# A new task list for the first thousand steps of an RWKV-7 + GELU kernel

## The chip, the cores and the metric

The kernel runs on one core of one Trainium2 chip, in one launch. The metric is the device time of that core in microseconds (us); lower is better.

## The reference

Two blocks follow each other. First an RWKV-7 recurrence over 768 time steps, for 4 batches x 8 heads of width 40, all in float32; then its output, as 3072 tokens of width 320, goes through a feed-forward block with a quick GELU between two matrix products (320 to 2048 and back).

```python
for t in range(S):                       # S = 768; B, H, D = 4, 8, 40
    y[:, :, t] = einsum('bhd,bhde->bhe', r_t, state)
    Sa = einsum('bhde,bhe->bhd', state, a_t)
    state = state * w_t - outer(Sa, b_t) + outer(v_t, k_t)
x = y.transpose(0, 2, 1, 3).reshape(B * S, H * D)
h = x @ w_in                             # 320 x 2048
out = (h / (1 + exp(-1.702 * h))) @ w_out  # 2048 x 320
```

## The kernel before

The time axis is cut into 12 chunks of 64 steps, and the four batches into two pairs. A chunk of one pair is a *unit*; there are 24, numbered 0 to 23, and units 2c and 2c+1 make up chunk c. Within a unit the recurrence becomes matrix products, and the work goes through these stages, all of them named by the tiles that they write:

- `decay(i)`: logarithms of the decays on ACT, sums over time as matmuls into `ps_cum` and `ps_cumc`, exponentials `FT`, `GT`, `wch`, `G` on ACT.
- `prep(i)`: the inputs `ak`, `b` and `time` are scaled by these (the results `ak`, `b`, `kh`, `bh`), on DVE or POOL; scores `A` and `RV` by matmul and a masked read out of PSUM on DVE.
- `inverse(i)`: a triangular inverse in five *levels*. For units 0 to 3 (`plain_level`), each level is a matmul into `ps_level`, a copy of the result `PT<-ps_level` (L792, ACT or DVE) and a transpose of the same PSUM tile `EX<-ps_level` (L729, DVE). Both must be done before the next level's matmul. Then come `ps_Q`, `QT`, `ps_T` and the inverse `T`.
- `solve(i)`: `ps_X`, the masked `M<-ps_X` (L915, DVE), `ps_y`; the new state `zraw` and the output `zr`; `x<-zr,FT` (L961, DVE or POOL). For units from 2 on, the state of unit i-2 enters through `zr<-zraw,wz`, `ps_zT` and `ps_rz`.
- `part_with` and `get_back` (L971, L975): `x` goes to DRAM and returns, turned, as `xT_all`.
- `mlp(c)`, once both units of chunk c are back: four groups q of ten steps `ps_up` (L300, 64x256 matmuls), a GELU `g<-ps_up` (L996, ACT) for each group, and for each of the two units eight steps `ps_down`.

The feed-forward weights come in eight blocks of 1.31 MB, each in four loads (L469), and each block is put through five steps before use: one on ACT (`rebased`, L447), three on DVE (`bounded` L451, `shifted` L455, `rounded` L459) and one on POOL (`joined`, L463). Blocks 0 to 3 are `w_in`: group q of chunk 0 waits for block q. Blocks 4 to 7 are `w_out`: steps 2n and 2n+1 of `ps_down` need block 4+n.

Nothing of the order is left to a scheduler. Every piece of work is a task with a number, the engines that may do it, a cost in ns on each of them (with the order written out these costs decide nothing, but they can be summed over a stretch of a list) and, where it uses PSUM, a pair of banks; `ORDER` is a text that lists all 2700 tasks, each with a letter for the engine (p TensorE, a ACT, d DVE, g POOL, s SyncE) and the number of its PSUM pair (0 to 3). `Plan.listed` reads it and the tasks are then issued one after the other, so each engine has its instructions in the order of the list:

```python
n, bank = one.split(ENGINES[e])
t = self.tasks[int(n)]
assert e in t.engines and t.after <= done and (e == "SP" or (t.pair is None) == (not bank))
t.engine, t.bank = e, int(bank or 0)
```

Every matmul of the kernel is recorded under one line (L300, a helper), so that TensorE's work is told apart by tile names. DMAs are all issued by SyncE, in the order of the list; a load of a unit's input waits there until the buffer of unit i-2 is free.

Of the kernel before, what the change touches and what calls it, by code (L numbers as in the profile page):

```python
# [119 lines left out]
214p1 389p2 66d 472a3 483g 204p0 390a2 560s 371p3 67d 306a 53s 215p1 71s 482s 216p1 372a3 217p1 476a 220p2 373d3 68g 218p1  # L120
221p2 477d 219a1 205p0 222p2 206p0 223p2 224p2 207p0 55a 311p3 225p2 79s 312d3 80s 226p2 208a0 58d 313p1 374p3 314d1 227p2 56d
379a3 228p2 229p2 57d 326p0 230a2 59g 393p1 327d0 378a3 391p2 394a1 375d3 231p0 558s 392d2 376a 232p0 233p0 395d1 559s 81s 73a
78s 234p0 480s 381p2 235p0 328p1 481s 382a2 74d 377a3 485d 380a3 236p0 75d 492a 242p2 486d 243p2 82a 76d 484d 77g 383p3 237p0
384d3 244p2 329d1 330d1 488p3 473d 238p0 531d 245p2 487g 246p2 489d3 85d 532p1 239p0 533a1 396p3 331d 332s 474s 475s 534a1
240p0 247p2 397d3 562s 241a0 535p1 83d 490p3 536a1 84d 398p0 572a 491d3 86g 550p1 555s 561s 253p3 399d0 551a 333s 400d0 254p3
401d 402s 554s 255p3 552a1 564d 493p0 705s 556a 567g 570p1 403s 494d0 248p2 563d 566g 249p2 495d0 498d 256p3 571d1 565g 250a2
496a0 251d2 252s 696p1 497g 557d 539p0 537p2 704s 257p3 538a2 540d0 258p3 553d 611d 697a 499d 573p2 784s 700s 259p3 576a2
574d2 710d 260p3 541d0 575d2 404p0 578d 261a3 577g 405p0 579d 698a1 568p2 711g 500p1 406p0 569d2 501a1 407p0 262d3 263s 708s
580p2 702a 502d1 408p0 582d2 409p0 503d 410p0 583d 504a 612p3 411p0 584g 613d3 412p0 614d3 413p0 505p1 709d 414a0 426p3 506d1
427p3 428p3 507d1 429p3 699d 581d2 430p3 615p1 785s 706s 701s 703d 431p3 616a1 585p0 432p3 508d 586a0 433p3 587d0 434p3 509a  # L130
588d 435p3 589d 448p2 436a3 510p1 590p0 511a1 449p2 592d0 591a0 512d1 415p3 513d 416p3 593d 514a 417p3 594g 418p3 515p0 419p3
516a0 517d0 595p1 518d 420p3 596a1 597d1 421p3 598d 422p3 519a 599d 423p3 424p3 520p0 425a3 437p1 521d0 438p1 523d0 522g 439p1
524d0 440p1 525d0 441p1 442p1 526d0 527p3 718p0 929s 528a3 443p1 719d0 787s 444p1 720d0 529p3 445p1 721d0 446p1 530d3 600p0
723d 447a1 542p3 722d 724g 603d0 605a0 619p1 604d0 543d3 450p2 620a1 606d0 544p3 621d1 601d0 602d 617p1 707s 546d3 451p2 618a1
783s 712d 547g 713d 607p0 725p1 608a0 452p2 609p0 453p2 548s 610d0 932s 454p2 727d1 726d1 622p0 728d 545d3 729a 775p1 455p2
623d0 780s 776a 549s 756d 730p3 624p0 456d2 457d2 731d3 458s 459p2 777a1 778g 732d3 786s 788g 781a 779s 626d0 460p2 625d0 627g
733d 795p1 835d 734a 461p2 735p3 791g 462p2 628s 736a3 796d1 737d3 716p0 792g 738d 463p2 782d 739g 1011s 920p1 757p3 925s
464p2 717d0 758a3 629s 759a3 790d 465p2 740p0 789d 466p2 741a0 742d0 921a 797p3 467d2 760p0 1008s 468d2 800a3 923d 652p2 469s
761d0 922a1 653p2 926a 930s 798d3 714p1 799d3 654p2 924s 802d 801g 655p2 934d 803a 656p2 836p0 657p2 715d1 658p2 659p2 837d0
762p3 838d0 927d 660p2 763a3 661p2 764p1 662a2 743d 630p0 744d 928s 631p0 632p0 765d1 804p3 766d1 633p0 805a3 806d3 634p0 807d  # L140
635p0 808a 745p2 636p0 748d2 637p0 749d2 839p1 933g 750d2 638p0 840a1 1009s 751d2 639p0 809p3 746d2 935g 640a0 641p1 810d3
642p1 793p2 747a 811d3 674p0 812d 794d2 813a 752p3 643p1 753a3 814p2 644p1 815a2 816d2 754p3 645p1 755d3 646p1 817d 647p1 818a
767p2 841p3 768d2 648p1 842a3 649p1 819p2 650p1 820a2 821d2 675p0 769p3 822d 651a1 823d 771d3 931s 770d3 772g 824p2 936d 676p0
827a2 828a2 942p1 829a2 677p0 1153s 830a2 937d 945a1 773s 663p3 825d2 664p3 943d1 1156s 826a 665p3 944d1 999p2 947d 946g 666p3
1000a 1004s 980d 940p1 948g 667p3 941d1 668p3 774s 669p3 670p3 831p1 671p3 1001a2 1002d 1003s 832d1 672p3 1005a 1013d 678p0
673a3 1006d 833p2 843p1 679p0 834d2 1007s 844d1 938p2 845d1 680p0 939d2 846p3 681p0 847d3 949p1 1012g 682d0 848p2 950a1 683d0
1014d 684s 685p3 849d2 1015g 1010s 850d2 1021p0 1016g 951d1 686p3 1024a0 1232s 851d 1235s 981p2 687p3 982a2 952d 852s 1022d0
983a2 953g 1144p1 1023d0 688p3 1026d 1145a 1149s 1025d 1027g 984p2 1059d 689p3 1154s 954p0 853s 985a2 1147g 690p3 1158d 1148s
955a0 956d0 986p2 1146a1 957d 1150a 691p3 958d 987a2 1151d 988p0 692p3 989a0 1152s 990d0 959p1 693a3 865p2 960a1 694d3 866p2
961d1 867p2 695s 962d 868p2 963d 1028p0 869p2 1029a0 1030d0 870p2 1031d 1157g 871p2 1159d 1032a 1060p3 872p2 873p2 1061a3  # L150
874p2 1062d3 1033p1 875a2 854p0 1035d1 855p0 1036d 856p0 1037d 1063p3 857p0 1064d3 1034a1 858p0 964p2 859p0 965a2 966d2 1038p1
967d 860p0 1039a1 1040d1 861p0 1041d 1017p3 968a 1042g 862p0 1018d3 863p0 969p2 864a0 876p1 970d2 877p1 972d2 971g 1043p3
973d2 878p1 1044a3 974d2 879p1 975d2 880p1 881p1 1045d3 1019p0 1046d 976p2 1047a 882p1 1020d0 1233s 883p1 977a2 1166p3 884p1
1169a3 1167d3 1377s 978p0 885p1 1168d3 898p2 1171d 1170g 886a1 979d0 887p3 1172a 1048p0 991p1 1051a0 888p3 1052a0 992d1 889p3
1053a0 890p3 1054a0 891p3 1049d0 993p1 1050a 1067p0 994d1 1160g 1155s 892p3 1161d 1068a0 893p3 894p3 1069d0 1380s 895p3 1204d
1065p0 995d1 896p3 996d 1066a0 1231s 1055p1 899p2 897a3 1056d1 997s 1173p0 1223p3 900p2 1174a0 1175d0 1228s 1176d 1224a 1177g
1057p1 901p2 1058d1 1070p0 998s 1164p1 1225a3 1226d 1236g 1227s 1071d0 902p2 1229a 1165d1 1162p3 903p2 1238d 1163d3 904p2
1237d 1178p0 1230d 905p2 1179a0 1180d0 1245p1 906a2 1181d 1072p3 1248a1 1456s 907d2 1182g 1246d1 908s 1247d1 909p0 1250d 1234s
1239g 1073d3 1251a 910p0 1240g 1074d3 1249d 1183p2 1459s 1283d 1368p1 911p0 1184a2 1075d 1373s 912p0 1185d2 1369a 1076s 1186d
# [978 lines left out]
```

## Time and profile before

| | |
|---|---|
| median of 3 runs | 678.03 us (677.79 to 678.33) |
| span of the profiled execution, first to last instruction | 676.5 us |
| PE (TensorE matmul) busy | 648.5 us, 96% of the span |
| DVE, ACT, POOL busy | 444.6, 331.6, 175.3 us |
| bytes moved by DMA | 69.74 MB, 103 GB/s over the span |

The page gives the span alone for the profiled execution; the runs' median is 1.5 us above it, and this much is taken to lie around the span. PE's matmuls overlap in the array and their ends are modelled, so that a busy share of 96% is no statement on the array's use; PE's idle time, on the other hand, is real. "issue" as the end of a wait means that the profile shows nothing that was waited for. All line numbers are those of the kernel before.

### The profile page before, as it was taken

The page shows a single profiled execution, that of the slowest core. Times are in us where ns is not written, and L with a number is a line of the kernel's source. Part 1 is how long each engine was busy: PE and PEld are TensorE (multiplying, and loading weights), DVE is VectorE, ACT ScalarE, POOL GpSimd, SP SyncE. Part 2 cuts the span into 40 slices and gives each one's busy share as a digit, 9 for nine tenths or more (in the row PEclk, how much of TensorE's full clock was granted, in tenths as well). Part 3 has the DMA queues.
Part 4 walks back from the last instruction along what each step waited for, and adds up shares of the span by engine and source line. Part 5 has one row for each costly group of instructions (what it writes and reads, how often), then busy time and mean ns, then how long its engine had stood idle before and what let it go on. Part 6 is the DMA issues. An engine that isn't in the chain of part 4 may idle for free.

```text
span 676.5 us, 42217 instructions
## 1 busy us (share of the span) xinstructions
PE 648.5 (96%) x19488; PEld 553.4 (82%) x19488; DVE 444.6 (66%) x908; ACT 331.6 (49%) x710; POOL 175.3 (26%) x204
## 2 busy tenths in 40 slices
PE   5768999999999999999999999999999999999997
PEld 5657887987998987788888888798888798798785
DVE  4786787777867667767776587768656766675001
ACT  4676755534564655664545445455454354252110
POOL 6344244224123123123123211322412421300000
PEclk9899999999999999999999999999999999999999
DMA  7983736315314314432404413513412411200200
GB/s 230 300 289 94 232 107 187 103 43 154 108 47 149 93 58 117 121 108 72 118 22 132 141 34 109 156 33 108 140 39 71 122 53 54 61 14 15 61 12 20
DMA packets 35313, 69.74 MB, mean 103 GB/s; under 512 B 5440, under 2 KB 14656, under 8 KB 35136
## 3 DMA queue, kind: packets, MB, share of 16 engines
q1 hardware_dynamic: 35136, 67.03, 32.6%
q8 instruction: 153, 2.51, 1.5%
q14 instruction: 24, 0.20, 0.1%
HBM read 59.15 MB, written 7.86 MB: 99 GB/s over the span
## 4 chain that ended last, share of the span: by engine, by line
PE 93%; DMA 2%; DVE 2%; issue 1%; ACT 1%; DVEq 0%; SPq 0%; ACTq 0%
PE ps_up L300 31%; PE ps_down L300 30%; PE ps_level L300 9%; PE ps_y L300 5%; PE ps_B L300 5%; PE ps_X L300 2%; PE ps_N L300 2%; PE ps_rz L300 2%; PE ps_RV L300 2%; PE ps_A L300 2%; PE ps_zT L300 1%; DMA ak<-in_ak 1%; PE ps_cum L300 1%; PE ps_T L300 1%; DMA b<-in_b 1%
## 5 line engine op out<-in xcount | busy, mean ns | idle before, releaser
L300 PE MATMUL ps_up<-xT_all,w_sb 64*64 64x256 f32 x3840 | 251.0, 377 | 0.8 <-issue 0.4
L300 PE MATMUL ps_down<-w_sb,g 64*64 64x320 f32 x3072 | 237.0, 430 | 0.2 <-ACT zr L877 0.2
L300 PEld LDWEIGHTS ps_up<-xT_all,w_sb 64*64 64x64 f32 x3840 | 170.1, 133 | 15.9 <-issue 1.5
L300 PEld LDWEIGHTS ps_down<-w_sb,g 64*64 64x64 f32 x3072 | 128.0, 133 | 42.8 <-ACT zr L877 0.4
L996 ACT ACTIVATE g<-ps_up 128x1024 f32<-128x1024 f32 x48 | 49.2, 1024 | 45.4 <-PE ps_up L300 45.0
L715 POOL TENSOR_TENSOR EX<-ES,quads 128x512 f32<-128x512 f32 x29 | 38.3, 1322 | 112.7 <-DVE ES L708 74.9
L300 PEld LDWEIGHTS ps_level<-W,EX 64*64 64x64 f32 x2560 | 57.8, 134 | 6.7 <-DVE T L838 0.5
L758 ACT COPY W<-ps_level 128x512 f32<-128x512 f32 (+1 forms) x56 | 29.5, 527 | 67.7 <-PE ps_level L300 65.7
L760 DVE TENSOR_TENSOR E<-two,ps_level 128x256 f32<-128x256 f32 x80 | 33.1, 415 | 34.2 <-ACT W L758 30.1
L300 PE MATMUL ps_level<-W,EX 64*64 64x64 f32 (+1 forms) x2560 | 55.4, 217 | 0.1
L713 ACT ACTIVATE EX<-ES,quads 128x256 f32<-128x256 f32 x80 | 36.3, 501 | 31.0 <-DVE ES L708 30.3
L619 POOL TENSOR_TENSOR ak<-ak,FT 128x512 f32<-128x512 f32 x16 | 20.9, 1305 | 76.6 <-DMA ak<-in_ak 53.4
L708 DVE STREAM_TRANSPOSE ES<-E 128x256 f32<-128x256 f32 x80 | 35.3, 443 | 4.4
L300 PE MATMUL ps_level<-PT,EX 64*64 64x64 f32 (+2 forms) x1280 | 32.8, 235 | 5.1 <-DVE EX L729 3.7
L300 PEld LDWEIGHTS ps_level<-PT,EX 64*64 64x64 f32 x1280 | 30.8, 139 | 8.3 <-DVE EX L729 4.2
L300 PE MATMUL ps_y<-M,bh 64*64 64x104 f32 (+1 forms) x768 | 35.6, 250 | 0.7 <-DVE M L915 0.4
L300 PE MATMUL ps_y<-RV,kh 64*64 64x104 f32 (+1 forms) x768 | 35.6, 251 | 0.0
L899 ACT COPY B<-ps_B 128x416 f32<-128x416 f32 (+1 forms) x34 | 16.6, 492 | 33.4 <-PE ps_B L300 33.2
L300 PEld LDWEIGHTS ps_y<-RV,kh 64*64 64x64 f32 x768 | 28.3, 137 | 2.6 <-DVE M L915 0.5
L689 DVE COPY_PREDICATED PT<-within,ps_N 128x256 f32<-128x256 uint32 x40 | 17.8, 444 | 18.5 <-ACT P L697 13.5
L915 DVE TENSOR_TENSOR M<-ps_X,later 128x832 f32<-128x832 f32 (+1 forms) x24 | 23.8, 993 | 8.3 <-PE ps_X L300 8.1
L300 PE MATMUL ps_B<-RV,A 64*64 64x104 f32 (+1 forms) x768 | 27.9, 252 | 1.1 <-issue 1.1
(131 smaller groups left out, 1088.2 us busy)
## 6 DMA issues: line engine op xcount, KB each, us to landing
ak<-in_ak SPq DMA_DIRECT2D x48, 160.0 KB
rv<-in_rv SPq DMA_DIRECT2D x48, 160.0 KB
time<-in_time SPq DMA_DIRECT2D x24, 320.0 KB
xT_all<-x_dram SPq DMA_DIRECT2D x48, 160.0 KB
wc<-in_wc SPq DMA_DIRECT2D x20, 264.0 KB
logw<-in_w SPq DMA_DIRECT2D x24, 160.0 KB
RV<-in_v SPq DMA_DIRECT2D x24, 160.0 KB
b<-in_b SPq DMA_DIRECT2D x48, 80.0 KB
```

The lines of the kernel that those rows point to most:

```text
L300: nc.tensor.matmul(o, lhsT, rhs, start=start, stop=True, skip_group_check=True)
L619: plan.add(R, {"DVE": 690.0, "POOL": 1270.0, "sbuf": True}, lambda t: of(t.engine).tensor_mul(ahT(), ahT(), FT_of(i)), reads=T("ak", "FT") ...
L689: plan.add(R, dve(256), lambda t, n=n: nc.vector.copy_predicated(tiles_of(at(E0_t, i)), every(within_of(n), [128, 2, 4, 32]), blocks(psum( ...
L708: plan.add(rank, dve(256), lambda t: nc.vector.transpose(ES(n), source(t)), writes=[key("ES", n, 6)], **reads)
L713: nc.scalar.activation(dst[:, :, h], ES(n), ACT.Copy, scale=quads[:, h, :1])
L715: of(t.engine).tensor_mul(dst, ES(n).unsqueeze(2).to_broadcast([128, 8, 2, 32]), quads.unsqueeze(1).to_broadcast([128, 8, 2, 32]))
L758: plan.add(rank, any2(512 - 8 * past), lambda t: copy(t.engine)(tiles_of(W(n + 1))[:, :, :, past:], blocks(psum(t, ""), 64)[:, :, :, past: ...
L760: plan.add(rank, dve(256), lambda t: nc.vector.tensor_sub(tiles_of(E(n + 1)), every(two32, [128, 2, 4, 32]), blocks(psum(t, ""), 64)[:, :, ...
L899: plan.add(R, any2(4 * wide), lambda t: copy(t.engine)(dst(), some(psum(t, "")[:, :, :208])), writes=[("Bv", i)] if x and c > 0 else T("B" ...
L915: plan.add(R + 1, dve(8 * wide), lambda t: nc.vector.tensor_tensor(M_of(i)[:, :, :wide].rearrange("p (j b) n -> p b j n", b=2), some(psum( ...
L996: plan.add(-45, {"ACT": 1030.0, "table": "gelu"}, lambda t: nc.scalar.activation(g_of(c * NQ + q).rearrange("p m r n -> p r m n"), psum(t, ...
```

## The change

Only the text `ORDER` differs; the tasks, their instructions and the code that issues them are the same. In the list:

- the first 999 of the 2700 entries are a new order of the same 999 tasks; the remaining 1701 are the same tasks on the same engines in the same order;
- 120 of the first 999 tasks are on another engine: 52 from ACT to DVE, 32 from DVE to ACT, 15 from DVE to POOL, 12 from POOL to DVE, 8 from ACT to POOL, 1 from POOL to ACT;
- the PSUM pairs of the first part are given out anew; in the rest, pairs 1, 2 and 3 are renamed to 2, 3 and 1 throughout;
- the SyncE entries move too, so the loads come in another order. Of the weights' 32 loads, 19 stood ahead of `ps_y` of unit 1 (entry 192p) and 9 do now; ahead of the first `ps_up` (entry 209p) 22 stood and 11 do.

The text has seven lines more, so a line below it is found seven lines further down (the matmul helper L300 is L307 there). The beginning of both lists, up to unit 0's first levels (matmuls 107p, 110p; copies `PT` 108, 111; transposes `EX` 109d, 112d):

```diff
-0s 5s 7s 8s 9s 3a 6s 87p0 88p1 24s 89a1 1s 2s 12s 102a 95d 100p2 90a0 93d 158a 101d2 98p3 96g 10s 94d 17s 97g 16s 99d3 103p1
-4a 11s 132p0 104a1 105d1 142p2 26s 143p3 133a0 106d 130p1 14s 144a3 13s 107p0 15s 18s 151g 108a0 109d0 51s 131a1 110p3 27s
-149g 150d 111a3 112d3 159p0 156p1 145a2 161d0 160a0 152g 113p3 345s 92a 162d 25s 153d 114a3 163p2 42s 115d3 34s 19a 274s 264p0
...
+0s 3a 87p2 88p3 89a3 90a2 158a 102a 9s 96g 5s 97g 93d 95d 7s 6s 100p0 8s 94d 101d0 1s 98p3 11s 18s 99d3 103p2 105d2 4a
+143p0 106d 142p1 10s 14s 144a0 149g 107p3 151g 104a2 108d3 109d3 145a1 2s 153g 110p3 150d 152g 111d3 112d3 159p2 161d2
```

In the old list `ps_y` of unit 1 is 192p, and 194a (`zr`), 195g (`x`), 196s (`part_with`), 197s (`get_back`) and the first `ps_up`, 209p, follow it; the lines of both lists with these:

```diff
-284d0 41g 285p3 185d1 344s 148a 286d3 190p0 293a2 294d2 334p1 335p3 357a 140s 191d0 268g 336a3 315d 192p2 47d 337a1 348d 316p0
-194a2 295p3 349d 61s 317a0 195g 60s 347s 358p1 296a3 62s 297d3 360d1 318a0 298p3 271a 361d 319p0 338g 300d3 196s 193a2 320a0
...
-388a2 323p1 367d0 366a0 321p3 49d 324a1 304p2 322a3 478s 325d1 50g 353p0 309a2 470p3 354d0 209p1 307a2 210p1 310a2 305d2 211p1
...
+316p1 44s 293a0 318a1 335p2 281g 317a1 334p0 336a2 29d 30d 192p3 194a3 295p1 343s 193a3 337a0 31d 348g 349d 140s 297d1
+347s 319p2 320a2 346s 358p3 296d1 321p0 338g 345s 195g 42s 360d3 359a3 361d 298p2 385d 299d2 362p3 32g 300d2 364d3 21d
...
+386p1 322a0 388a1 301p2 323p0 23g 352g 387a1 302a2 363d3 196s 303d2 324d0 365p3 355p2 141s 325d0 36s 304p1 197s 389p0
+356d2 305d1 209p2 366a3 492a 271a 308d1 307d1 33s 34s 390a0 351d 210p2 350g 211p2 309a1 35s 212p2 213p2 367d3 272d 470p0
```

More of the change, by code (lines that the diff above doesn't have):

```diff
@@ L120 @@
[L120 to L159, printed above, removed]
@@ new lines @@
+1764p0 1930d1 1864g 1956p3 1765p0 1931d1 1957a3 1766p0 1932d 1958a3 1767p0 1933d 1865p2 1768p0 1868a2 1934p1 1869a2
+1769p0 1935d1 1770p0 1870a2 1794p3 1871a2 1936d1 1937d 1771a0 1866d2 1772p1 1938d 1867g 1959p2 1773p1 1960a2 2129s
+1939p0 1774p1 1940a0 1941d0 1775p1 1942d 1872p2 1776p1 1943d 1873a2 1777p1 2062p0 1778p1 2065a0 2063d0 2273s 1874p2
+1779p1 1875d2 1780p1 2064d0 1781p1 2067d 1887p2 1782a1 2066d 2068g 1783p0 1888d2 1784p0 1961p1 1944p2 1962a1 1785p0
+1945d2 1889p1 1947d2 1946a 1948d2 1949d2 1786p0 2051s 1950d2 1787p0 1891d1 1963p2 1890d1 1892g 1788p0 2127s 1964d2
@@ new lines @@
+2267g 2278d 2106p2 1810p1 2271d 2107a2 2268s 2108p0 1811p1 2109a0 2272s 2110d0 2148p3 1812p1 2149a3 2150d3 2151d 2180p2
+1813a1 2137p0 2181d2 2152a 1974p3 1814d1 1975p3 2138d0 1976p3 2182a2 1815s 2277g 1977p3 2279d 1978p3 1979p3 1980p3
+2183p1 1981p3 2184a1 2351s 1982p3 1983p3 2153p2 1984a3 1985p0 2154d2 1986p0 1987p0 2155d2 2079p1 2156d 1988p0 2157d
+2080a1 1989p0 2081d1 2018p2 2082d 2083a 2158p3 1990p0 2160d3 1991p0 2161d 2084p1 2159d3 2162a 1992p0 1993p0 2085d1
+1994p0 2086d1 2163p3 1995a0 2087d 1996p1 2164d3 2088g 1997p1 1998p1 2165d3 1999p1 2166d 2000p1 2167a 2089p0 2001p1
@@ new lines @@
+2360d0 2210p2 2405p1 2211p2 2406d1 2566s 2212p2 2375p0 2213p2 2376a0 2377d0 2214p2 2378d 2215p2 2379a 2308p3 2216p2
+2310d3 2309a3 2217p2 2311d 2218p2 2312d 2380p1 2219a2 2220p0 2381d1 2221p0 2222p0 2382d1 2313p3 2383d 2223p0 2384a
+2314d3 2224p0 2316d3 2315g 2225p0 2317d3 2385p2 2318d3 2226p0 2386a2 2319d3 2227p0 2228p0 2387d2 2320p1 2388d 2504p3
+2389d 2321a1 2229p0 2242p2 2507a3 2505d3 2230a0 2506d3 2509d 2508g 2231p1 2510a 2322p3 2390p0 2323d3 2232p1 2393d0
+2335p3 2394d0 2233p1 2395d0 2234p1 2396d0 2235p1 2336d3 2236p1 2237p1 2391d0 2407p3 2392a 2337p0 2408d3 2409p3 2339d0
@@ new lines @@
+2517a3 2262d0 2420p2 2586d1 2421p2 2263s 2422p2 2518d3 2617p0 2519d 2423p2 2618a0 2587d1 2520g 2424p2 2619a0 2588d
+2425p2 2589a 2620p3 2426p2 2621d3 2521p1 2427p2 2522a1 2523d1 2428p2 2524d 2429p2 2525d 2590p0 2430a2 2431p3 2591d0
+2432p3 2433p3 2592d0 2526p1 2593d 2434p3 2594d 2527a1 2435p3 2528d1 2436p3 2529d 2437p3 2530a 2595p0 2438p3 2596d0
+2439p3 2440p3 2597d0 2531p2 2598d 2441a3 2442p1 2599d 2443p1 2532d2 2444p1 2534d2 2533a 2600p0 2535d2 2445p1 2446p1
+2536d2 2601a0 2447p1 2537d2 2448p1 2602d0 2538p3 2603d 2449p1 2604d 2539a3 2450p1 2451p1 2540p2 2605p0 2452a1 2541d2
@@ L245 @@
+2656p1 2657p1 2658p1 2659p1 2660p1 2661p1 2662p1 2663p1 2664p1 2665p1 2680p0 2666a1 2667p2 2668p2 2669p2 2670p2 2671p2
+2672p2 2673p2 2674p2 2675p2 2676p2 2681p0 2677a2 2682p0 2683p0 2684p0 2685p0 2689p3 2686d0 2687d0 2690p3 2688s 2691p3
+2692p3 2693p3 2694p3 2695p3 2696p3 2697d3 2698d3 2699s
 """
```

206 lines of the change are left out of this document (115 added, 91 removed).

## The prediction

> **What bounds the kernel now.** I read the page's busy shares first, then the same by stage, cut where the list has its marks: the first `ps_up` of chunk 0 (67.55 us), that of chunk 1 (119.28), and the last of the 999 entries that the change reorders (237.30).
>
> ```profile
> span 676.5 us, 42217 instructions
> PE 648.5 (96%) x19488; PEld 553.4 (82%) x19488; DVE 444.6 (66%) x908; ACT 331.6 (49%) x710; POOL 175.3 (26%) x204
> PE   5768999999999999999999999999999999999997
> q8 instruction: 153, 2.51, 1.5%
> ```
>
> ```profile
> 0.00:67.55 67.55, 46.27 (x1712) 41.62 (x1716) 45.53 (x76) 41.48 (x110) 32.85 (x61) 0.95 0.72 228
> 67.55:119.28 51.73, 50.34 (x1361) 42.47 (x1353) 41.06 (x66) 31.36 (x68) 19.32 (x11) 1.00 0.56 175
> 119.28:237.30 118.02, 117.75 (x3674) 104.14 (x3678) 86.18 (x183) 64.40 (x131) 31.35 (x35) 1.00 0.33 98
> 237.30:676.50 439.20, 434.16 (x12756) 365.22 (x12748) 271.78 (x587) 194.39 (x403) 91.79 (x98) 1.00 0.26 77
> ```
>
> The columns are length, then busy time of PE, its weight loads, DVE, ACT and POOL, then granted clock, DMA share and GB/s. PE idles for 21.3 us (67.55 less 46.27) before the first `ps_up`, for 1.4 in the next stage, 0.3 in the third; the 5.0 of the last lie in entries whose order and engines stay. PE's matmuls are the same in both lists, so only time in which PE stands still, or runs at a low clock, can be won, and that is before 67.55. The question is when the first `ps_up` starts, and whether the stage behind it stays full.
>
> What PE waits for in the first 76 us:
>
> ```profile
> PE ps_level L300 <- DVE EX L729: 3.7, 3, 1.7
> ...
> PE ps_cum L300 <- issue: 2.1, 1, 2.1
> ...
> PE ps_B L300 <- issue: 1.1, 1, 1.1
> ...
> PE ps_rz L300 <- issue: 0.8, 1, 0.8
> ...
> PE ps_level L300 <- issue: 0.6, 2, 0.3
> ...
> PE ps_A L300 <- issue: 0.5, 1, 0.5
> PE ps_up L300 <- issue: 0.4, 1, 0.4
> ...
> PE ps_y L300 <- issue: 0.3, 1, 0.3
> ```
>
> (waits in us: total, times, longest). Two kinds: DVE's transposes `EX` of the levels, and 5.8 us of "issue", for which the profile shows no releaser. I take these for waits for instructions: queue q8 brings PE and the others 2.51 MB in 153 packets, 16 KB each, beside the loads.
>
> DVE's own account between its first scaling of `ak` and the masked read `M` of unit 1, and what it waits for there:
>
> ```profile
> 6.68:48.90 42.22, 30.09 (x1067) 26.53 (x1068) 30.25 (x50) 27.51 (x75) 20.57 (x23) 0.96 0.91 292
> ```
>
> ```profile
> DVE EX L729 <- ACT PT L792: 6.9, 6, 2.9
> ...
> DVE RV L650 <- PE ps_RV L300: 1.7, 2, 1.3
> DVE PT L722 <- ACT P L697: 1.6, 1, 1.6
> DVE b L621 <- DMA b<-in_b: 0.5, 2, 0.3
> DVE ES L708 <- ACT Tc L805: 0.5, 1, 0.5
> DVE A L638 <- PE ps_A L300: 0.4, 1, 0.4
> ```
>
> DVE is busy for 30.25 of 42.22 us and waits for 12.0, of which 6.9 are `EX`, waiting for ACT's copy `PT` of the same PSUM tile: the two read one after the other, and the matmul of the next level waits for both. So a level costs ACT's queue, the copy, then the transpose. DVE is the engine to follow to `M`(1).
>
> ```profile
> 6.68 0.69 DVE L624 TENSOR_TENSOR ak<-ak,GT 128x512 f32<-128x512 f32 x1 [2.00 <-ACT GT L565]
> 48.90 0.98 DVE L915 TENSOR_TENSOR M<-ps_X,later 128x832 f32<-128x832 f32 x1
> 50.21 0.51 PE L300 MATMUL ps_cum<-logw,edges 64*64 64x160 f32 x3 [2.13 <-issue]
> 53.82 0.42 PE L300 MATMUL ps_y<-M,bh 64*64 64x104 f32 x8
> 58.84 2.90 SPq L975 DMA_DIRECT2D xT_all<-x_dram  x4
> 67.55 0.41 PE L300 MATMUL ps_up<-xT_all,w_sb 64*64 64x256 f32 x4
> ```
>
> (start, length.) `ps_y` of unit 1 ends at 54.24; `x` goes out and is fetched back, with the fetch issued until 61.74; the first `ps_up` starts at 67.55.
>
> **The change part by part.** *Ahead of `M`(1) on DVE.* The old list has nine of the weights' scalar steps ahead of it, the new one two; the 768-wide copies `PT` go the other way, none of them on DVE before and six now.
>
> ```profile
> L451 DVE TENSOR_SCALAR w_sb<-w_sb x8: 783/818/1889, 26.2 to 102.1; 128x1280 f32<-128x1280 f32 x8
> ```
>
> ```profile
> L758 DVE COPY W<-ps_level 128x512 f32<-128x512 f32 x19 | 13.0, 683 | 4.8 <-PE ps_level L300 4.4
> L915 DVE TENSOR_TENSOR M<-ps_X,later 128x832 f32<-128x832 f32 x22 | 22.5, 1021 | 8.3 <-PE ps_X L300 8.1
> ```
>
> Seven steps at the median of 0.82 us take off 5.7. No row has a 768-wide copy on DVE; the nearest are a 512-wide copy at 0.68 and an 832-wide two-input read at 1.02. I take 0.95, near the wider; six add 5.7 (4.1 to 6.1). Other small steps that change sides, by the list's costs, come to -0.6, give or take 1. Busy: 30.25 - 5.7 + 5.7 - 0.6 = 29.6.
>
> The waits: with copy and transpose both on DVE, `EX` no longer waits for ACT's queue but for DVE's own step before it, so its 6.9 us should go; but matmul, copy and transpose of one unit stay a chain, and DVE must have the other unit's work to fill in. I keep half, 3.5 (bounds 0 and 6.9), and the other 4.7 whole. `M`(1) starts at 6.68 + 29.6 + 4.7 + 3.5 = 44.5 (41.0 to 47.9), 4.4 earlier. That DVE's start at 6.68 stays is my assumption: the head of the list has the same loads, `logw` and scaling there, turned round among themselves.
>
> *From `M`(1) to `y`(1).* Its end at 49.88 to 54.24 is 4.36 us, with a 2.13 us "issue" wait inside and a slow clock:
>
> ```profile
> 50.00:60.00 10.00, 8.30 (x333) 8.00 (x336) 5.83 (x9) 6.50 (x18) 4.75 (x8) 0.83 0.23 71
> ```
>
> With another order another matmul meets that wait, and I keep half of what these cost: 2.9 us, so `y`(1) ends at 45.5 + 2.9 = 48.4, 5.8 earlier (4.4 with nothing saved). The Trainium skill, "Runtime: NRT & Kernel Launch", section "Instruction fetch mechanics", says that instructions come in blocks of 16 KiB ahead of use, at a cost that is mostly hidden; by it there would be no such wait, and `y`(1) would end 0.7 us earlier still. The 5.8 us of "issue" above speak against it here.
>
> *From `M`(1) to the first `ps_up`.* Again DVE's account:
>
> ```profile
> 49.88:67.55 17.67, 14.50 (x605) 13.57 (x608) 11.05 (x19) 10.97 (x29) 7.35 (x9) 0.90 0.33 98
> ```
>
> ```profile
> DVE EX L729 <- ACT PT L792: 2.5, 1, 2.5
> DVE ak L619 <- ACT FT L565: 1.6, 1, 1.6
> DVE A L638 <- PE ps_A L300: 1.4, 1, 1.4
> ```
>
> 11.05 us busy and 6.6 idle, nearly all of it these three. By the list's costs DVE has 1.8 us more in this stretch: three more of the `PT` copies, less the steps that moved. 12.85 busy, and of the waits 3.0, somewhat under half, since the 2.5 is again a `PT` on ACT: the first `ps_up` at 45.5 + 12.85 + 3.0 = 61.4, 6.15 earlier. The way of `x` allows it: `get_back` was issued until 7.5 us after `y`(1)'s end and 5.8 before `ps_up`; from 48.4 that gives 55.9, 5.5 before it. Loads: 22 of the weights' pieces lay ahead of the first `ps_up` and 11 do now, so the transfers of the first stage, which filled 0.91 of the DMA engines, have less ahead of the inputs; I count no gain for that beyond the waits above.
>
> *Behind the first `ps_up`.* What was taken from the front comes back here: by the list's costs, from the first `ps_up` of chunk 0 to that of chunk 1, DVE goes from 39.2 to 45.9, POOL from 17.5 to 33.1, PE from 49.2 to 50.4. DVE measured 41.06 there, so 47.9 now, 95% of PE's 50.4. How full DVE can run:
>
> ```profile
> 30.00:40.00 10.00, 6.64 (x277) 5.51 (x268) 9.37 (x16) 6.51 (x18) 5.97 (x4) 1.00 0.99 327
> ```
>
> At 93% DVE needs 51.5, so PE loses 1.1 (0 to 3). Beyond, nothing changes but the names of pairs.
>
> *Sum.* -6.15 + 1.1 = -5.05: span 676.5 to 671.5, and with the 1.5 us by which the median of 678.03 stands above the span, **673.0 us**. About 0.2%, 1.4 us, is what a measurement of this kernel can tell from no change.
>
> **The rivals.** *A larger gain.* With the `EX` waits gone and no "issue" wait on the way, `M`(1) starts at 41.0 rather than 44.5, and the later waits shrink as well; and the clock, 0.96 and 0.83 in the two windows above, cost 1.7 us in each, some of which a steadily busy PE would win. That is 5 us more ahead, -10: 668. For it: most of these waits have one cause, which the list takes away. Against: PE idle 21.3 us cannot all go, since inputs have to arrive.
>
> *No change.* The order of loads and of matmuls decides where the instruction waits fall. If those 5.8 us double and lie on the path, or a weight's block that now comes later is late for its group of `ps_up` by as much, the 5.05 are gone: 678. Against: fewer loads stand ahead in the queues.
>
> *Slower.* DVE and POOL at once. One of the eight steps at L451 took 1.89 us instead of 0.82; it started at 74.24, just when POOL began
>
> ```profile
> 74.17 1.27 POOL L619 TENSOR_TENSOR ak<-ak,FT 128x512 f32<-128x512 f32 x1 [6.26 <-ACT FT L578]
> ```
>
> and was held for that op: 1.07 us lost. In the new list POOL has twice the work behind the first `ps_up`, and DVE has the weights' SBUF steps there. Ten hits cost 10.7: DVE 58.6 us against PE's 50.4, which loses 8.2 instead of gaining 6.15: +2.05, 680. It decides from some eight hits on (47.9 + 8.6 = 56.5, PE loses 6.1, nothing is left). By the Trainium skill, "SBUF — State Buffer", section "Who interferes with whom", a VectorE step with two SBUF inputs or in a two-port mode and a GpSimd step exclude each other for the whole instruction; by that rule the row is the rule and no accident. Against ten hits: POOL was at work for about half of the first stage (32.85 of 67.55 us), and still the median of those eight steps is 0.82.
>
> That the change does not do what it says cannot be: the list is read entry by entry.
>
> **How the numbers follow.** The forecast, 0.58, whose own terms move it by the 3.5 of `M`(1)'s bounds to either side; the larger gain 0.20; no change 0.08; slower 0.14. Faster by over 0.2% (below 676.7) takes the first two, 0.78; within 0.08; slower (above 679.4) 0.14. The range goes from 667, below the larger gain, to 679, above no change; it leaves out the slower case and a rest of the larger gain, together not much over 0.15.
>
> **What would show it.** Right: the first `ps_up` between 59 and 63, `M`(1) at 42 to 46, the waits of `EX` for `PT` on ACT a few tenths instead of 6.9, PE's idle from there to the next chunk's first `ps_up` 1 to 3 us, and the third and fourth stage as long as before. Wrong: `M`(1) no earlier than 47.9; the first `ps_up` early but PE waiting for DVE, POOL or weights behind it; L451 to L459 often near 1.9 us; or "issue" waits of 10 us in the first 76.

## The result, and the profile after

The new list is slower: 695.27 us (692.73 to 698.31, 4 runs) against 677.91 (676.62 to 678.33) beside it, a ratio of 1.025 with an interval of 1.022 to 1.029. The forecast was 673.0, with a range of 667 to 679. The profiled execution took 692.73 us, its span is 691.0; the sums below are made against the old span of 676.5, a difference of 14.5.

The page of the new kernel (busy shares, then PE in 40 slices), and its stages, cut at the first `ps_up` of chunk 0 (66.12 us), of chunk 1 (132.01) and at the end of the reordered entries (250.54); columns as before:

```profile
span 691.0 us, 42208 instructions
PE 652.6 (94%) x19488; PEld 555.0 (80%) x19488; DVE 465.2 (67%) x920; ACT 312.9 (45%) x673; POOL 192.8 (28%) x220
PE   4767897999999999999999999999999999999997
```

```profile
0.00:66.12 66.12, 44.67 (x1704) 40.87 (x1705) 48.76 (x74) 28.02 (x88) 33.68 (x66) 0.95 0.62 190
66.12:132.01 65.89, 55.38 (x1438) 44.16 (x1434) 56.76 (x79) 33.63 (x65) 38.10 (x23) 0.97 0.53 171
132.01:250.54 118.53, 117.81 (x3613) 101.05 (x3609) 85.68 (x182) 57.01 (x118) 29.33 (x36) 1.00 0.33 103
250.54:691.00 440.46, 434.77 (x12756) 368.91 (x12748) 274.00 (x588) 194.28 (x403) 91.64 (x98) 1.00 0.26 76
```

The first `ps_up` comes 1.43 us earlier, not 6.15. The loss is in the second row: 65.89 us instead of 51.73, for PE work that the list's costs put at 50.4 us (49.2 in the old order, where some steps stand on the other side of the cut). I call stage length less PE's cost its *growth*: 15.5 us against 2.5. (Summed from the start of the run, this is PE's *lag*.) That is 13.0 more; 2.7 more come later, in two stages in which the old kernel's PE loses little.

What PE waits for in the second stage (new kernel, total, times, longest):

```profile
PE ps_RV L307 <- DVE A L645: 2.7, 1, 2.7
PE ps_up L307 <- issue: 1.9, 1, 1.9
PE ps_A L307 <- DVE zraw L949: 1.6, 1, 1.6
PE ps_X L307 <- DVE T L845: 1.3, 2, 1.1
PE ps_level L307 <- DVE W L765: 1.2, 1, 1.2
PE ps_level L307 <- issue: 1.0, 1, 1.0
PE ps_level L307 <- DVE EX L736: 0.4, 1, 0.4
```

7.2 us are for DVE. The timelines of DVE and POOL around the two longest waits (start, length):

```profile
102.12 3.59 DVE L458 TENSOR_SCALAR w_sb<-w_sb 128x1280 f32<-128x1280 f32 x1
...
109.19 0.47 DVE L949 TENSOR_TENSOR zraw<-ps_y,zr 128x320 f32<-128x320 f32 x1
...
110.51 3.37 DVE L541 TENSOR_TENSOR_SCAN wc<-starts,wc 128x264 f32<-128x264 f32 x1
113.81 0.66 DVE L645 TENSOR_TENSOR A<-ps_A,upper 128x512 f32<-128x512 f32 x1
```

```profile
101.74 3.28 POOL L470 TENSOR_TENSOR w_sb<-w_sb,extra 128x1280 int32<-128x1280 int32 x1
...
109.99 3.33 POOL L470 TENSOR_TENSOR w_sb<-w_sb,extra 128x1280 int32<-128x1280 int32 x1
```

A step of 0.82 us takes 3.59 and a scan of 0.68 takes 3.37; they end 0.69 and 0.56 us after POOL's `joined` is over, about the time that they take alone. `A`, for which PE waits, stands right behind the scan in DVE's queue, and `zraw` some steps behind the other. Over the whole stage 16 DVE steps are over 0.15 us longer than the median of their kind, 14.5 us in sum, while POOL is at work; in the old kernel's stage 6 steps, 5.6 us. I call this sum the *holds*. Only five of the 16, with 5.8 us, are the weights' scalar steps; the others are scans, `x`, `wz`, `zr` and `b`, steps that read two inputs from SBUF. The Trainium skill, "SBUF — State Buffer", section "Who interferes with whom", has a VectorE step of these kinds and a GpSimd step shut each other out for the whole instruction; these rows agree.

A second loss in that row is no wait: the granted clock is 0.97, and 1.00 in the old kernel's stage. Nearly all of it lies in one place:

```profile
110.00:120.00 10.00, 7.33 (x164) 4.82 (x162) 8.45 (x9) 2.27 (x6) 5.78 (x5) 0.83 0.05 17
```

That is 1.7 us (0.17 of 10), an estimate. It comes right behind the longest wait, that for `A`, which ended at 114.52: sixteen `ps_down` matmuls from 115.36 on took 2.38 us, for which the list's cost is 1.08. So of the 13.0 us some 9.1 are idle time of PE (65.89 less 55.38, against 51.73 less 50.34), 1.7 the clock, and 2.2 lie in PE's busy time and are not explained.

The "issue" waits have grown too. In both kernels nearly all the longer ones come at the same place of a block of 256 PE instructions (the 186th to 204th) and end 1.2 to 1.7 us after a 16 KB packet of the instruction queue has landed; I call them *block waits*. That PE waits for instructions there is inferred from this place and this time alone. Counted from the start of one instruction to the start of the next, there are 13.1 us of them up to chunk 1's first `ps_up`, in 15 waits, against 8.0 in 11; the "issue" rows, which count idle time alone, have 10.3 us in 10 and 5.9 in 8.

### The profile page after: what moved, and what is told of

Same layout as the page of the kernel before. It is cut to its first block, busy times and chain, and to the rows that moved or that the text cites. A ratio compares the mean times of both kernels' runs of the same rounds, so it can differ in the third digit from the quotient of the medians.

```text
span 691.0 us, 42208 instructions
## 1 busy us (share of the span) xinstructions
PE 652.6 (94%) x19488; PEld 555.0 (80%) x19488; DVE 465.2 (67%) x920; ACT 312.9 (45%) x673; POOL 192.8 (28%) x220
## 4 chain that ended last, share of the span: by engine, by line
PE 83%; DVE 7%; issue 4%; DMA 4%; POOL 1%; ACT 1%; SPq 0%; DVEq 0%; POOLq 0%
PE ps_down L307 28%; PE ps_up L307 27%; PE ps_level L307 8%; PE ps_y L307 5%; PE ps_B L307 4%; PE ps_X L307 2%; PE ps_RV L307 1%; PE ps_rz L307 1%; PE ps_A L307 1%; PE ps_N L307 1%; PE ps_zT L307 1%; PE ps_T L307 1%; DVE PT L799 1%; DVE EX L736 1%; PE ps_cum L307 1%
## 5 line engine op out<-in xcount | busy, mean ns | idle before, releaser
L307 PE MATMUL ps_up<-xT_all,w_sb 64*64 64x256 f32 x3840 | 246.2, 377 | 2.1 <-issue 2.1
L307 PE MATMUL ps_down<-w_sb,g 64*64 64x320 f32 x3072 | 239.8, 431 | 0.2 <-ACT zr L884 0.2
L307 PEld LDWEIGHTS ps_up<-xT_all,w_sb 64*64 64x64 f32 x3840 | 166.5, 133 | 22.5 <-issue 3.0
L307 PEld LDWEIGHTS ps_down<-w_sb,g 64*64 64x64 f32 x3072 | 135.5, 134 | 39.5 <-issue 1.5
L722 POOL TENSOR_TENSOR EX<-ES,quads 128x512 f32<-128x512 f32 x32 | 42.5, 1329 | 146.3 <-DVE ES L715 90.6
L1003 ACT ACTIVATE g<-ps_up 128x1024 f32<-128x1024 f32 x48 | 49.2, 1025 | 46.4 <-PE ps_up L307 46.1
L307 PEld LDWEIGHTS ps_level<-W,EX 64*64 64x64 f32 x2560 | 57.8, 134 | 5.8 <-DVE T L845 0.4
L307 PE MATMUL ps_level<-W,EX 64*64 64x64 f32 (+1 forms) x2560 | 56.1, 218 | 0.0
L765 ACT COPY W<-ps_level 128x512 f32<-128x512 f32 (+1 forms) x49 | 26.3, 536 | 58.7 <-PE ps_level L307 52.7
L307 PEld LDWEIGHTS ps_level<-PT,EX 64*64 64x64 f32 x1280 | 31.5, 139 | 13.6 <-issue 7.5
L307 PE MATMUL ps_level<-PT,EX 64*64 64x64 f32 (+2 forms) x1280 | 33.7, 237 | 8.8 <-DVE EX L736 3.8
L626 POOL TENSOR_TENSOR ak<-ak,FT 128x512 f32<-128x512 f32 x14 | 18.7, 1333 | 67.7 <-DMA ak<-in_ak 36.9
L307 PE MATMUL ps_y<-RV,kh 64*64 64x104 f32 (+1 forms) x768 | 36.1, 252 | 0.1
L307 PE MATMUL ps_y<-M,bh 64*64 64x104 f32 (+1 forms) x768 | 35.8, 252 | 0.0
L634 POOL TENSOR_TENSOR kh<-time,G 128x320 f32<-128x320 f32 x19 | 16.6, 874 | 53.2 <-PE ps_y L307 27.9
L307 PEld LDWEIGHTS ps_y<-RV,kh 64*64 64x64 f32 x768 | 29.2, 137 | 2.7 <-DVE M L922 0.6
L307 PEld LDWEIGHTS ps_B<-RV,A 64*64 64x64 f32 x768 | 25.4, 137 | 4.7 <-issue 0.7
L307 PE MATMUL ps_B<-RV,A 64*64 64x104 f32 (+1 forms) x768 | 28.3, 252 | 0.9 <-issue 0.5
```

Of the source, the lines that this page charges most:

```text
L307: nc.tensor.matmul(o, lhsT, rhs, start=start, stop=True, skip_group_check=True)
L626: plan.add(R, {"DVE": 690.0, "POOL": 1270.0, "sbuf": True}, lambda t: of(t.engine).tensor_mul(ahT(), ahT(), FT_of(i)), reads=T("ak", "FT") ...
L634: plan.add(R + 4, {"POOL": 870.0, "DVE": 490.0, "sbuf": True}, lambda t, n=n, dst=dst: of(t.engine).tensor_mul(dst(i)[:, :, :D], by_head(t ...
L722: of(t.engine).tensor_mul(dst, ES(n).unsqueeze(2).to_broadcast([128, 8, 2, 32]), quads.unsqueeze(1).to_broadcast([128, 8, 2, 32]))
L765: plan.add(rank, any2(512 - 8 * past), lambda t: copy(t.engine)(tiles_of(W(n + 1))[:, :, :, past:], blocks(psum(t, ""), 64)[:, :, :, past: ...
L1003: plan.add(-45, {"ACT": 1030.0, "table": "gelu"}, lambda t: nc.scalar.activation(g_of(c * NQ + q).rearrange("p m r n -> p r m n"), psum(t, ...
```

## The experiments

Names with a_ start from the new list, with b_ from the old one. Each ratio is to runs of the old kernel on the same chip, where it took 677.9 us beside the new kernel and 679.9 to 681.5 beside the others. Growth, holds, block waits and clock are from one profile each, summed as above; the new kernel's two profiles (new, after_again) give 15.5 and 16.9 for the growth and 4.6 and 8.3 for the block waits, so differences of 1 or 2 us in the one, and of 3 or 4 in the other, say little. A clock under 1.00 is part of the growth: what is missing, times the stage's length, is an estimate of its share, 1.7 us in the new kernel and nearly 7 in b_weights_as_after.

| kernel | ratio to the old kernel (interval) | first `ps_up` | growth | holds | block waits in that stage | clock in that stage |
|---|---|---|---|---|---|---|
| old | 1 | 67.6 | 2.5 | 5.6 | 2.2 | 1.00 |
| new | 1.025 (1.022 to 1.029) | 66.1 | 15.5 | 14.5 | 4.6 | 0.97 |
| after_again | 1.026 (1.023 to 1.029) | 65.4 | 16.9 | 15.3 | 8.3 | 0.97 |
| a_weights_as_before | 1.031 (1.029 to 1.033) | 75.8 | 11.2 | 13.2 | 1.3 | 0.97 |
| b_weights_as_after | 1.026 (1.022 to 1.029) | 67.0 | 20.2 | 13.8 | 2.5 | 0.90 |
| a_joined_in_4 | 1.024 (1.022 to 1.027) | 69.2 | 10.5 | 10.9 | 0 | 0.96 |
| b_joined_in_4 | 1.004 (1.002 to 1.005) | 69.4 | 2.5 | 6.3 | 1.5 | 1.00 |
| a_joined_thin | 1.021 (1.014 to 1.029) | 66.9 | 9.1 | 6.9 | 6.0 | 1.00 |
| b_joined_thin | 1.002 (0.999 to 1.005) | 70.3 | 3.2 | 1.6 | 2.3 | 1.00 |
| a_pool_as_before | 1.022 (1.016 to 1.029) | 71.6 | 13.0 | 10.9 | 3.9 | 0.94 |
| a_loads_5_to_7_out | 1.025 (1.019 to 1.031) | 66.0 | 13.9 | 15.8 | 2.2 | 0.97 |
| a_four_moved | 1.028 (1.023 to 1.032) | 66.6 | 16.4 | 11.8 | 6.3 | 0.95 |
| b_to_209_then_a | 1.020 (1.017 to 1.023) | 71.2 | 9.3 | 12.6 | 1.4 | 0.97 |
| a_to_404_then_b | 1.029 (1.025 to 1.034) | 67.0 | 18.8 | 15.8 | 3.0 | 0.93 |
| a_pool_light | 1.022 (1.017 to 1.028) | 69.2 | 7.4 | 3.2 | 4.6 | 1.00 |
| a_pool_light_loads_out | 1.019 (1.014 to 1.023) | 71.6 | 4.9 | 3.2 | 1.7 | 1.00 |
| b_PT_as_after | 1.007 (1.004 to 1.010) | 72.1 | 1.2 | 5.3 | 0.6 | 1.00 |
| a_engines_as_before | 1.042 (1.036 to 1.048) | 69.0 | 14.8 | 13.8 | 4.4 | 1.00 |
| b_engines_as_after | 1.016 (1.009 to 1.022) | 76.6 | 2.9 | 7.3 | 1.2 | 1.00 |

### The weights' entries alone, both ways

The first lines of the two lists (the loads 24s, 17s, 16s and 18s are the weights'):

```diff
 a_weights_as_before
-0s 3a 87p2 88p3 89a3 90a2 158a 102a ... 1s 98p3 11s 18s 99d3
+0s 3a 87p2 88p3 24s 89a3 90a2 158a 102a ... 1s 98p3 17s 16s 11s 99d3
 b_weights_as_after
-0s 5s 7s 8s 9s 3a 6s 87p0 88p1 24s 89a1 ... 98p3 96g 10s 94d 17s 97g
+0s 5s 7s 8s 9s 3a 6s 87p0 88p1 89a1 ... 98p3 18s 96g 10s 94d 97g
```

> The new list, but the weights' entries (32 loads, and the steps on ACT, DVE and POOL) stand at the place that they have in the old list, counted in PE entries; the other entries keep the new order and engines. Theory 'place' (the 14.5 us are lost because the weights' DVE and POOL steps were put behind the first ps_up, where DVE is full and POOL holds it): 678 to 682 us, DVE's excess over its medians behind the first ps_up back from 14.5 to about 6 us. Rival 'order' (the rest of the new order and its engines cost the time): stays at 692 to 697. Rival 'blocks' (PE's waits for instruction blocks, 13 us in the new kernel before 130 us, 5.8 in the old): stays above 688, since PE's order is untouched.

> The old list, but the weights' entries stand at the place that they have in the new list, counted in PE entries (three entries wait a little longer for what they need). Theory 'place': slower by 8 to 16 us, 686 to 694. Rivals 'order' and 'blocks': within 3 us of 678.

701.13 and 697.33 us: both slower. Putting the weights behind costs the old order 17.7 us of growth (20.2 against 2.5, nearly 7 of it by the clock) and brings its first `ps_up` forward by only 0.6. This half of "place" holds, and its time is above what was expected. But the new order does not recover with the weights in front: it pays there (75.8 us to the first `ps_up`) and still grows by 11.2 behind it. In b_weights_as_after PE's waits of that stage begin with one that the old kernel does not have, for a weights' block that is late:

```profile
PE ps_down L300 <- POOL w_sb L463: 4.7, 1, 4.7
PE ps_rz L300 <- DVE EX L729: 2.5, 1, 2.5
```

### POOL's joined in four quarters

```diff
-            nc.gpsimd.tensor_tensor(out=scale(), in0=scale(), in1=word(INT32, 1), op=ALU.add)
+            [nc.gpsimd.tensor_tensor(out=scale()[:, s], in0=scale()[:, s], in1=word(INT32, 1)[:, s], op=ALU.add) for s in (slice(g * PIECE // 4, (g + 1) * PIECE // 4) for g in range(4))]
```

> The new list, with POOL's step joined of each weights' block as four instructions over a quarter of the columns instead of one over all. Same work, but each holds the port for 0.75 us instead of 3.0. Theory 'ports' (DVE's SBUF steps wait for the end of a POOL instruction): DVE's excess behind the first ps_up falls from 14.5 to 7 to 9 us, its longest SBUF step from 3.6 to under 1.8, and the time by 3 to 6 us. Rival (DVE simply has too much work there): within 1.5 us of the new kernel. If DVE never gets in between two quarters, the excess stays as well.

> The old list with the same cut of joined. Theory 'ports': a hit of 1.9 us (the scan at 78.78 us) shrinks to under 0.8, but PE hardly waits for DVE there: within 1.5 us of 678. The rival expects the same.

696.01 and 682.31 us. Growth fell by 5.0, to 10.5, holds to 10.9 and the longest held step from 3.59 to 1.89 us: the way that "ports" said, but short of its numbers (7 to 9, and under 1.8). The time did not fall at all: the first `ps_up` came 3.1 us later, behind 12.8 us of block waits, and the rest of the run lost more (below). The old kernel lost 2.4 us; in its profile 1.8 are lost ahead of the first `ps_up` and more behind chunk 1's. The quarters are no cure: POOL is held in its turn.

```profile
L470 POOL TENSOR_TENSOR w_sb<-w_sb,extra x20: 869/1270/2832, 62.4 to 113.9; 128x320 int32<-128x320 int32 x20
```

(Shortest, median and longest in ns.)

### joined on a tenth of its columns

```diff
-            nc.gpsimd.tensor_tensor(out=scale(), in0=scale(), in1=word(INT32, 1), op=ALU.add)
+            nc.gpsimd.tensor_tensor(out=scale()[:, :128], in0=scale()[:, :128], in1=word(INT32, 1)[:, :128], op=ALU.add)
```

> The new list, with POOL's step joined done on 128 of its 1280 columns (the rest of each block's rounding is left out). DVE keeps every step; only POOL's 3.0 us instructions become short. Theory 'ports' (behind the first ps_up PE waits for DVE steps that POOL's instructions hold): DVE's excess there from 14.5 to under 8 us, the two PE waits of 2.7 us (for the masked A) and 1.6 us (for zraw) gone, and the time down by 5 to 9 us, 686 to 690. Rival 'too much DVE work': DVE's work is the same, so within 2 us of 695. Rival 'blocks': also within 2 us.

> The control: the old list with joined on 128 of 1280 columns. All theories: 676 to 680, since PE waits little for DVE behind the first ps_up; if the short joined alone won 5 us here too, the new kernel's gain with it would say nothing on its list.

695.04 (691.61 to 701.71) and 682.03 us. The stage did what "ports" said. Its row, and PE's waits for DVE in it:

```profile
66.93:126.49 59.56, 53.87 (x1439) 43.72 (x1435) 47.68 (x79) 33.41 (x65) 20.51 (x22) 1.00 0.59 188
```

```profile
PE ps_level L307 <- DVE W L765: 1.3, 1, 1.3
...
PE ps_RV L307 <- DVE A L645: 0.2, 1, 0.2
```

With the same 79 DVE steps DVE is busy for 47.68 us instead of 56.76, the wait for `A` is 0.2 instead of 2.7, the one for `zraw` is gone, and growth is 9.1 instead of 15.5. The control's growth stays (3.2). The time that was forecast for the whole run, 686 to 690, did not come: what the stage won, 6.4 us (1.7 of it the clock), the stretch behind chunk 1's first `ps_up` lost again (its lag grows by 12.5 us there, by 6.4 in the new kernel's profile). But in after_again, the new kernel itself, it grows by some 12 too, so that this loss may belong to the execution and not to the variant. The interval of the ratio, 1.014 to 1.029, leaves a gain of up to some 8 us open.

### POOL's entries, old engines

Entries whose engine is POOL in one of the lists, put back (36), for example:

```diff
-376g
+376a
-485g
+485d
-483d
+483g
```

> The new order, with the 36 entries whose engine is POOL in one list and another in the other put back on their old engine; all else as in the new list. Theory 'ports': POOL's busy time behind the first ps_up falls from 38 to under 30 us and the hits by those steps go (the excess from 14.5 to 9 to 12), while some DVE work comes back (x, ak, EX): 688 to 694. Rival 'too much DVE work': slower than the new kernel by 2 to 5 us.

696.01 us; growth 13.0, holds 10.9: within the expectation on holds, above it on time. The first `ps_up` came at 71.6, 5.5 us later than in the new kernel. DVE has only 0.7 us more work ahead of it (49.46 against 48.76); the block waits ahead of it are some 15 us, against 8.5.

### The loads behind the first ps_up

```diff
-            plan.add(rank, {"SP": 350.0}, lambda t, some=some: nc.sync.dma_start(raw()[:, some], src[:, some]),
+            plan.add(rank, {"SP": 350.0}, lambda t, some=some: n > 4 or nc.sync.dma_start(raw()[:, some], src[:, some]),
```

> The new list without the loads of the weights' blocks 5, 6 and 7 (12 of the 21 loads behind the first ps_up; the steps on these blocks work on what the buffer holds). Theory 'blocks' (PE waits for its next instructions because their packets queue behind loads): the waits of this kind behind the first ps_up fall from 4.6 to under 2 us, and the time by 2 to 4. Theory 'ports': within 1.5 us of the new kernel, as the hits stay.

699.16 us. Block waits fell from 4.6 to 2.2 us and growth by 1.6, near what "blocks" said for the stage, but not beyond what two profiles of one kernel differ by; the time did not fall.

### The new kernel again, and six DVE steps moved

```diff
-... 74d 383p3 76d ... 384d3 82a
+... 74d 383p3 ... 384d3 76d 82a
-... 486d 83d 494d0 341a 559s 85d 84d 495d0 ... 533a2 399d3 488p3 ... 342d 333s 551a 489d3
+... 486d 494d0 341a 559s 495d0 ... 533a2 399d3 83d 85d 84d 488p3 ... 333s 489d3 342d 551a
-... 502d2 503d 504g ... 477d ... 501d2
+... 502d2 503d 501d2 504g ... 477d
```

> The new kernel itself, beside the others on one chip. 692 to 699 us; the lag of PE behind its own work grows by 13 to 16 us from the first ps_up of chunk 0 to that of chunk 1 (by 2.2 in the old kernel).

> The new list with six of DVE's 920 steps at another place in DVE's own order, in four moves; engines, and the order of PE, POOL, ACT and SyncE, as in the new list. The three SBUF steps on weights' block 7 go behind the read zraw of unit 3, the two scans of unit 5 behind the masked read A of unit 4, one weights' step behind T of unit 3, and a copy W ahead of the scans of unit 6: each is a read of PSUM that PE waits for and that stood behind a step held by POOL. Theory 'ports, where DVE is full' (held steps stand ahead of reads for which PE waits): PE's waits of 1.6 us for zraw, 2.7 for A, 1.1 for T and 1.2 for W shrink to under 0.5 each, and the time falls by 4 to 7 us against the new kernel on the same chip. Rival 'too much work on DVE': the same work in another order, so the waits come back within the stage and the time stays within 2 us.

698.77 and 698.74 us: no difference. PE no longer waits for `zraw`, `A` and `W`; but PE's waits in the stage now begin with

```profile
PE ps_rz L307 <- ACT G L598: 2.8, 1, 2.8
PE ps_up L307 <- issue: 2.7, 1, 2.7
PE ps_zT L307 <- issue: 1.9, 1, 1.9
```

The scans put back are held all the same (holds 11.8), ACT's exponentials (`FT` to `G`) wait for them, and PE for ACT. The rival came true here: while POOL holds DVE, moving these reads only chose which chain is late.

### One list's head, the other's rest

```diff
 b_to_209_then_a: the old list up to 209p, then the new one's entries that are left
-... 209p1 307a2 210p1 310a2 305d2 211p1 ...
+... 389p0 305d2 209p1 492a 308d2 307d2 390a0 210p1 211p1 ...
 a_to_404_then_b: the new list up to 404p, then the old one's
-... 404p3 508d 584g 585p2 555s ...
+... 560s 555s 556a 570p1 571d1 557d 704s 611d 784s 710d 404p2 405p2 ...
```

(PSUM pairs are given out anew where they would meet.)

> The old list up to the first ps_up; then what is left, in the order and on the engines of the new list (34 of its entries have been done already, most of them weights'; two come later). Theory 'order behind' (the loss is in the new order between the two chunks' first ps_up, whatever ran ahead): PE's lag still grows by 8 us or more there, 686 to 692. Rival 'work put off' (the loss is the 32 entries that the new list does behind the first ps_up): the lag grows by under 4, 679 to 683.

> The new list up to the first ps_up of chunk 1, then the old order and engines. All theories that put the loss ahead of it: 690 to 697, 1 to 3 us below the new kernel. If more than 4 us come back, the engines of the stretch behind matter too.

694.31 and 701.39 us, both above the expected times. With 22 weights' loads and 20 of their steps ahead of the first `ps_up`, as in the old list, the new order still grows by 9.3, with holds of 12.6: its order costs it, not only the work put off. The old order behind 404 brings nothing back: at chunk 1's first `ps_up` PE's lag is already 16.0 us above the old kernel's, 4.2 more than in the new kernel. The ten old entries at the seam, where PE waits 2.2 us for an input, are part of that.

### Order or engines, POOL light, and the copies alone

```diff
 a_engines_as_before: 120 entries, as
-108d3
+108a3
 b_engines_as_after: the same entries, as
-108a0
+108d0
 a_pool_light: the 23 entries new on POOL back, as
-121g
+121a
 and joined on 128 columns, as above
 a_pool_light_loads_out: the same, and without the loads of blocks 5 to 7, as above
 b_PT_as_after: 13 entries, as
-108a0
+108d0
```

> The new order with all 120 entries back on their old engines. Theory 'order': 693 to 702, as slow as the new kernel or slower. Theory 'engines' (the new engines, POOL's above all, carry the loss): 680 to 688.

> The old order with all 120 entries on their new engines. Theory 'order': within 4 us of the old kernel, 679 to 685. Theory 'engines': 690 or more. If both this and the new order on the old engines are slow, the two fit only each other.

> The new list with the 23 entries that it gave to POOL back on DVE or ACT, and joined on 128 of 1280 columns (the rest of the rounding left out). Theory 'POOL' (its holds of DVE and its own queue, on which T, x and ak stand behind joined, make the loss behind the first ps_up): PE's lag grows there by 3 to 6 us instead of 15.5 (9.2 with the short joined alone), 683 to 689 us. Rival 'order' (the order of matmuls and DVE steps costs it whatever POOL does): growth stays at 8 us or more, 689 to 697.

> The new list with POOL light as before (its 23 new entries back on DVE or ACT, joined on 128 of 1280 columns) and without the loads of weights' blocks 5 to 7 (the steps work on what the buffer holds). Theory 'POOL and blocks' (what POOL does not cost there is waits for instructions whose packets come late among the loads): the lag grows by 3 to 5 us instead of 7.3, these waits fall from 4.6 to under 2.5. Rival 'order' (the rest is the order itself): it grows by 7 again.

> The old list with only the 13 copies PT<-ps_level that change engines on the new list's engine (12 from ACT to DVE, one back). The forecast's step by itself: DVE's waits for ACT's PT (6.9 and 2.5 us) gone, 6 copies at 0.96 us more on DVE ahead of M of unit 1: 0 to 3 us faster, M(1) at 46 to 49 us, 676 to 681. Rival: DVE, with its weights' steps still ahead of M(1), gets later instead: 1 to 4 us slower, 682 to 686.

707.87, 690.92, 695.12, 693.42 and 684.62 us. The new order on the old engines grows by 14.8; the old order on the new engines by 2.9, and loses its time ahead of the first `ps_up` (76.6, 9.0 us later) and behind chunk 1's. By the whole runs' times both are slow, and order and engines fit only each other; by stages it is the order that counts behind the first `ps_up`. POOL is busy for 27.0 us in the stage in both, but the holds are 13.8 us in the new order and 7.3 in the old. The stage of the old order with the new engines:

```profile
76.58:128.73 52.15, 50.27 (x1360) 43.72 (x1353) 42.97 (x69) 28.79 (x57) 26.96 (x18) 1.00 0.56 172
```

DVE has 9 us to spare there, and PE hardly notices the holds; the new order has DVE at 56.76 of 65.89. With POOL light, and then without the loads as well:

```profile
69.16:126.97 57.81, 52.71 (x1438) 47.63 (x1434) 46.13 (x85) 35.63 (x71) 10.47 (x13) 1.00 0.61 194
```

```profile
71.56:126.88 55.32, 52.55 (x1438) 46.04 (x1433) 46.02 (x85) 35.78 (x71) 10.28 (x13) 1.00 0.40 116
```

Growth goes 15.5, 9.1 (short `joined`), 7.4 (POOL's new entries off it), 4.9 (loads out); the old kernel has 2.5. 7.4 lies between what the two theories gave (3 to 6, and 8 or more); the last run, within its numbers, puts 2.5 of it on loads in the way of instructions, as far as one profile each can. The time of a_pool_light, 695.12, was above the 683 to 689 that "POOL" expected. That DVE simply has too much work of its own does not explain the 15.5: with POOL light it has 85 steps instead of 79, and the stage is 8 us shorter.

Over all kernels of the table growth goes with DVE's busy time in the stage, holds included: at most 3.2 us where DVE is busy for 37 to 43 us, 4.9 to 9.3 at 46 to 48, 11.2 at 50, and 10.5 to 20.2 at 53 to 58, for 49 to 51 us of PE work. So growth goes with how full DVE is, held steps included; this alone proves no cause.

The copies `PT` alone made the old kernel slower by 0.7%: DVE's row up to `M`(1), and its longest new wait:

```profile
6.68:52.54 45.86, 32.99 (x1072) 29.93 (x1075) 35.66 (x58) 22.65 (x68) 20.18 (x22) 0.85 0.83 259
```

```profile
DVE PT L792 <- PE ps_level L300: 2.8, 2, 1.8
```

5.4 us more of work (35.66 against 30.25), and waits of 10.2 instead of 12.0: the 6.9 for ACT went, others took most of their place.

## Why the prediction was wrong, point by point

**Where time can be won.** Right: only ahead of 67.55 us; and the forecast's check on the stage behind (PE losing 1 to 3 us) was the place that decided.

**`M`(1) at 44.5.** It came at 46.60, inside the bounds of 41.0 to 47.9. DVE's first scaling, the new kernel's row to `M`(1) (it begins 0.63 us ahead of that scaling), and DVE's waits:

```profile
7.24 0.69 DVE L626 TENSOR_TENSOR ak<-ak,FT 128x512 f32<-128x512 f32 x1 [2.55 <-DMA ak<-in_ak]
```

```profile
6.61:46.60 39.99, 28.32 (x1064) 25.74 (x1065) 30.05 (x48) 17.17 (x60) 17.69 (x28) 0.96 0.62 191
```

```profile
DVE PT L799 <- PE ps_level L307: 3.1, 2, 2.2
DVE ak L626 <- DMA ak<-in_ak: 2.5, 1, 2.5
DVE EX L736 <- PE ps_level L307: 1.7, 3, 1.0
```

The busy time was right (29.6 forecast, 30.05 measured; the copy 0.95, and 0.94 in the median). `EX` waits no more for ACT, as forecast; but a copy on DVE waits for the matmul instead (3.1), and `EX` with it (1.7): 4.8 where 3.5 was kept. The other waits, 4.7 in the sum, came to 4.5, but are others. And DVE did not start at 6.68, as was assumed, but at 7.24, after a wait for its input `ak`. So 7.24 + 30.0 + 9.3 gives 46.6. The experiment with the copies alone shows that without the weights' steps taken off, this term is a loss.

**From `M`(1) to `y`(1).** 2.9 us forecast, 5.3 measured (47.58 to 52.90): it holds the longest block wait of the front, 3.07 us. I had taken half of the old one; these waits grew, to 8.5 us ahead of the first `ps_up` from 5.8. Nor did the clock rise: 0.91 from there to `ps_up`, and 0.90 before.

**To the first `ps_up`.** 15.9 us forecast from the end of `M`, 18.54 measured:

```profile
47.58:66.12 18.54, 14.67 (x600) 13.61 (x600) 14.48 (x19) 7.18 (x22) 11.09 (x10) 0.91 0.64 199
```

DVE busy 14.48 instead of 12.85, with 2.0 us of holds, and idle 4.1 instead of 3.0. (The three waits that the prediction called nearly all of the old 6.6 us make 5.5.) Together: 1.43 us won instead of 6.15.

**Behind it.** The step that failed: +1.1 (0 to 3) was forecast, +13.0 came. DVE's load was 47.9 in the sum, which carried the old kernel's holds along unchanged, and 56.76 in fact. The rival "slower" had the mechanism and its size (58.6 for ten hits), at a chance of 0.14; the argument against it went by the median of the eight weights' steps at L451, and 11 of the 16 steps held now are no weights' steps at all. It also had the price too low: 8.2 became 15.5. Of these the experiments put about 8 on POOL (15.5 to 7.4, the 1.7 of the clock among them) and 2.5 on loads and block waits, and leave 2.4 more than in the old kernel. That PE lost more than DVE's sum was above PE's because held steps stood ahead of reads is the likely reason, from the waits for `A` and `zraw`; it is not shown, as moving these reads won nothing.

**Beyond.** "Nothing changes" was wrong by 2.7 us in the profile, and by 5 to 9 in most of the variants of the new list. Block waits are part of it (2.2 us in the new kernel, 8.2 in after_again, 0.7 in the old, some 8 in a_joined_thin and 6 in a_pool_light). From the one profile of the new kernel to the other they rise by 6.0 us, and the lag gained behind the stage by 5.6. Why the same entries meet more of them behind the new head was not settled, and so it stays open whether the stage's gains in a_joined_thin and a_pool_light were lost by the variants or by the executions that were profiled.

No version beat the old kernel.

## What to carry to other kernels

Load taken off the front of a pipeline has to be priced where it lands, with the contention of that place, not with the durations of the place it left: 16 held steps made 42 us of DVE work into 57. An engine with slack hid such holds (7.3 us of them left the growth at 2.9, where DVE was busy for 43 of 52 us); where it was nearly full, PE waited for reads behind held steps. And a read that was late because the engine's queue was held was not cured by moving it: the next chain was late instead.
